# Attention with normalized Q and K on one core: a new plan for three engines, with 64-row QK matmuls, VectorE's QK placed first and one tile more for VectorE

## Chip, core and metric

The kernel runs on one core of a Trainium2 chip. The metric is the device time in microseconds (us). The kernel before takes 748.66 us (median of 3 runs, 748.62 to 749.63). All comparisons are made with runs of the kernel before on the same chip, in the same rounds; between chips and rounds its mean lies between 748.7 and 749.7 us in this study, so a ratio says more than a time.

## The reference

```python
B, H, S, Dh = 1, 32, 2048, 20
def reference(q, k, v, t):
    qn = q / (jnp.sqrt((q * q).sum(axis=-1, keepdims=True)) + 1e-6)
    kn = k / (jnp.sqrt((k * k).sum(axis=-1, keepdims=True)) + 1e-6)
    logits = jnp.einsum('bhqd,bhkd->bhqk', qn, kn) * t[None, :, None, None]
    attn = softmax(logits, axis=-1)
    return jnp.einsum('bhqk,bhkd->bhqd', attn, v)
```

Inputs and output are bfloat16. The logits are bounded, so no maximum is taken. There are 32 x 2048 x 2048 exponentials, and they are the bulk of the work.

## The kernel before

The program builds a list of tasks with durations and dependencies, runs a list scheduler over it at build time, and emits each engine's instructions in the order that came out. On the chip each engine then works strictly in that order. So the durations in the plan never appear in the program; they only decide the order.

```python
SEM_LAT = {"PE": 0.18, "ACT": 0.15, "DVE": 0.10, "POOL": 0.15, "SP": 0.0}
...
if e == "PE":     # prefer the kind of matmul that ran last: a change of kind costs time
    x = min(ready[e], key=lambda r: (r[0] + (0.0 if r[2].name[:2] == last_pe[0] else self.SWITCH), r[1]))
```

The work of a head is 16 row tiles of 128 keys, each with four units of 128x512 logits. Most tiles are ScalarE's: three units make a wave in three PSUM banks (psA, double buffered), and one exp instruction of 128x1536 turns it into bfloat16 probabilities in the ring p_ring. Some tiles are VectorE's: it reads the logits of one unit at a time from the single bank psD (L532, four times per tile) and makes the exponential in integer arithmetic, in four wide instructions per tile (L540 to L546).

```python
DVE_TILES = [4 if h % 3 == 1 else 3 for h in range(H)]      # 107 tiles for VectorE
...
def add_wave(w):          # QK of three units: a 64-row pair, and a single at 128 rows
    pair = ...            # two units whose operands lie in different halves of the array
    qks = [add("PE", ..., lambda e, tk, part=part:
               f_qk(e, part, 32 if plain else 64 if part is pair else 128), ...,
               deps, due_a(us[0]) - 100) for part in parts]
    act[w] = add("ACT", f"exp{w}", ..., 0.065 + n / 1200.0, qks + war, w)   # n = 1536
...
def add_dgroup(jg):       # VectorE's tile: QK into psD, then L532, four times
    for g in reversed(range(NG)):
        qk = add("PE", f"qkD{j}.{g}", ... qk_mm(e, h, r, g, psD[:, :], 128 if j else 32),
                 PE_MM, dep, due - 0.5)
        t1_prev[0] = add("DVE", f"t1.{j}.{g}", ...)          # L532
```

The operand of a 128-row QK is padded with zeros (qz), so 64 and 128 rows give the same result. PV of both kinds of tiles accumulates in the single bank psO, four matmuls of 32 columns at a time. At the end of a head VectorE transposes psO (L446), and the next head's PV waits for that.

Of the kernel before, what the change touches and what calls it, by code (L numbers as in the profile page):

```python
# [27 lines left out]

class Task:
    __slots__ = ("eng", "fn", "dur", "deps", "pri", "name", "lat", "dma", "n", "users",  # L30
                 "start", "end", "seq", "inc", "cnt")

    def __init__(self, eng, name, fn, dur, deps, pri, lat=0.0, dma=None):
        self.eng, self.name, self.fn, self.dur = eng, name, fn, dur
        self.deps = [d for d in deps if d is not None]
        self.pri, self.lat, self.dma = pri, lat, dma
        self.inc, self.cnt = False, 0


class Program:  # L40



    SEM_LAT = {"PE": 0.18, "ACT": 0.15, "DVE": 0.10, "POOL": 0.15, "SP": 0.0}

    SWITCH = 0.3

    def __init__(self):
        self.tasks = []
# [5 lines left out]
        return t  # L55

    def schedule(self):
        for t in self.tasks:
            t.users = []
        for i, t in enumerate(self.tasks):  # L60
            t.seq = i
            deps = []
            for d in t.deps:
                deps += d() if callable(d) else [d]
            t.deps = list(dict.fromkeys(deps))
            t.n = len(t.deps)
            for d in t.deps:
                d.users.append(t)
        free = {}
        ready = {}  # L70
        events = []
        rt = {}

        def arrive(t, when):
            heapq.heappush(events, (when, 0, t.seq, t))

        for t in self.tasks:
            free.setdefault(t.eng, 0.0)
            ready.setdefault(t.eng, [])
            rt[t.seq] = 0.0  # L80
            if t.n == 0:
                arrive(t, 0.0)
        order = {e: [] for e in free}
        done = 0
        last_pe = [""]
        while events:
            now = events[0][0]
            touched = set()
            while events and events[0][0] <= now:
                _, kind, _, t = heapq.heappop(events)  # L90
                touched.add(t.eng)
                if kind == 0:
                    heapq.heappush(ready[t.eng], (t.pri, t.seq, t))
            for e in touched:
                if free[e] > now + 1e-9 or not ready[e]:
                    continue
                if e == "PE":
                    x = min(ready[e], key=lambda r: (r[0] + (0.0 if r[2].name[:2] == last_pe[0] else self.SWITCH), r[1]))
                    ready[e].remove(x)
                    heapq.heapify(ready[e])  # L100
                    t = x[2]
                else:
                    _, _, t = heapq.heappop(ready[e])
                t.start = now
                t.end = now + t.dur
                if e == "PE":
                    kind = t.name[:2]
                    if kind != last_pe[0]:
                        t.end += 0.09
                        self.nsw += 1  # L110
                    last_pe[0] = kind
                free[e] = t.end
                order[e].append(t)
                done += 1
                heapq.heappush(events, (t.end, 1, t.seq, t))
                for u in t.users:
                    lat = t.lat if t.dma else (0.0 if u.eng == e and e != "DVE" else self.SEM_LAT[e])
                    rt[u.seq] = max(rt[u.seq], t.end + lat)
                    u.n -= 1
                    if u.n == 0:  # L120
                        arrive(u, rt[u.seq])
        assert done == len(self.tasks), "dependence cycle"
        self.order = order
        return order
# [57 lines left out]
def bass_standalone__qk_norm__prompt_kernel(  # L182
# [20 lines left out]
    GD = 1  # L203
    WPLAIN = 5
    EARLY = 3
    NSOLO = 4
    LEAD = 2.1
    PE_MM = 0.23
    DVE_TILES = [4 if h % 3 == 1 else 3 for h in range(H)]

    with ExitStack() as es:  # L211
        sbuf = lambda name, shape, dt: es.enter_context(nc.sbuf_tensor(name, shape, dt))
# [107 lines left out]
        def add_prep(hs):  # L320
            due = hs[0] - LEAD
            n = len(hs)
            w = 2 * R * n

            def dv(name, fn, dur, deps):
                return add("DVE", name + str(hs[0]), fn, dur, deps, due)
            sums = []
            for i, h in enumerate(hs):
                x = qk_sb[h % NB]
                s1 = dv("sq", lambda e, tk, x=x: e.tensor_tensor(sq[:, :, :], x[:, :, :], x[:, :, :], ALU.mult),  # L330
                        0.86, lds[h] + last_sum)
                sums.append(dv("sum", lambda e, tk, i=i: e.tensor_reduce(  # L332
                    rs["sum"][:, 2 * R * i:2 * R * (i + 1)], sq[:, :, :], AXIS_X, ALU.add), 0.86, [s1] + prep_last[0]))
                last_sum[:] = sums[-1:]
            c = dv("rs", lambda e, tk: e.tensor_scalar(  # L335
                rs["u"][:, 0:w].bitcast(I32), rs["sum"][:, 0:w].bitcast(I32), -0.5, 1597463007.0, ALU.mult, ALU.add),
                0.11 + 0.03 * n, sums)
            cur = rs["u"]
            for tgt in (rs["y"], rs["r"]):
                c = dv("rs", lambda e, tk, cur=cur: e.tensor_tensor(  # L340
                    rs["a"][:, 0:w], cur[:, 0:w], cur[:, 0:w], ALU.mult), 0.09 + 0.03 * n, [c])
                c = dv("rs", lambda e, tk: e.scalar_tensor_tensor(
                    rs["b"][:, 0:w], rs["a"][:, 0:w], -0.5, rs["sum"][:, 0:w], ALU.mult, ALU.mult), 0.09 + 0.03 * n, [c])
                c = dv("rs", lambda e, tk, cur=cur, tgt=tgt: e.scalar_tensor_tensor(
                    tgt[:, 0:w], rs["b"][:, 0:w], 1.5, cur[:, 0:w], ALU.add, ALU.mult), 0.09 + 0.03 * n, [c])
                cur = tgt
            rq = rs["r"][:, 0:w].rearrange("p (n x) -> p n x", n=n)[:, :, 0:R]
            tq = t_f32[:, hs[0]:hs[0] + n]
            tq = bass.AP(tq.tensor, tq.offset, [tq.ap[0], [1, n], [0, R]])
            c = dv("rs", lambda e, tk: e.tensor_tensor(rq, rq, tq, ALU.mult), 0.08 + 0.03 * n, [c, tcp])  # L350
            if hs[0] == 0:
                first_head(c)
                prep_last[0] = [norm[0]] + rot[0][-1].deps
# [1 line left out]
            for i, h in enumerate(hs):  # L355
                x, b = qk_sb[h % NB], h % NN
                war = [trn[h - NN]] if h >= NN else [z_qkn[b]]
                norm[h] = dv("norm", lambda e, tk, x=x, b=b, i=i: e.tensor_tensor(  # L358
                    qkn[b][:, :, 0:D], x[:, :, :], bc(rs["r"][:, 2 * R * i:2 * R * (i + 1)], 2 * R), ALU.mult),
                    0.86, [c] + war)  # L360
            prep_last[0] = [norm[h] for h in hs]
            for h in hs:
                add_trn(h)
# [17 lines left out]
        def first_head(rinv):  # L381
# [1 line left out]
            kv = kx[:, :].rearrange("p (e c g w) -> p e c g w", e=4, c=4, g=4)  # L383
            nk = add("DVE", "normk0", lambda e, tk: e.tensor_tensor(
                kx[:, 0:512].rearrange("p (r w) -> p r w", w=32)[:, :, 0:D],
                x[:, R:2 * R, :], bc(rs["r"][:, R:2 * R], R), ALU.mult), 0.45, [rinv, z_kx], -3)

            rq = rs["r"][:, 0:R]
            nq = add("DVE", "normq0", lambda e, tk: e.tensor_tensor(
                qkn[0][:, 0:R, :].rearrange("p (c g) w -> p c g w", g=4)[:, :, :, 0:D],  # L390
                x[:, 0:R, :].rearrange("p (g c) d -> p c g d", c=4),
                bass.AP(rq.tensor, rq.offset, [rq.ap[0], [1, 4], [4, 4], [0, D]]), ALU.mult),
                0.45, [rinv, z_qkn[0]], -2.9)
            cp = []
            for dl in range(1, 4):
                for (g0, s0, m) in ((0, dl, 4 - dl), (4 - dl, 0, dl)):
# [46 lines left out]
        def add_fin(h):  # L443
# [2 lines left out]
            trO[h] = add("DVE", f"tr{h}", lambda e, tk: e.transpose(  # L446
                oT[:, :, :].rearrange("p r d -> p (r d)"), psO[:, :]), 0.63,
                [lambda: pv_users[h]] + ([fin[h - 1]] if h else []), -10 + due)
            rc = add("DVE", f"rec{h}", lambda e, tk: e.reciprocal(rec[:, :], oT[:, :, D]), 0.17, [trO[h]], due)
            st = o_stage[b2][:, :].rearrange("p (r d) -> p r d", d=D)  # L450
            src, rb = oT[:, :, 0:D], bc(rec[:, :], R)
            if h == 0:
# [1 line left out]
                src = oT[:, :, 0:D].rearrange("p (c m) d -> p c m d", m=4)  # L454
                rb = bass.AP(rec, 0, [rec[:, :].ap[0], [4, 4], [1, 4], [0, D]])
            fin[h] = add("DVE", f"fin{h}", lambda e, tk: e.tensor_tensor(st, src, rb, ALU.mult),
                         0.45, [rc] + (sto[h - 2] if h >= 2 else []), due)
            if h == 0:
                sto[h] = [dma("SP", "st0", bass.AP(out.tensor, out[0, 0].offset + 4 * g * D,
                                                   [[16 * D, 32], [512 * D, 4], [1, 4 * D]]),  # L460
# [10 lines left out]
        def add_wave(w):  # L471
# [17 lines left out]
            for h in hs:  # L489
                moved = any(A_units[u][0] == h and (A_units[u][1] - A_units[u][2]) % 4 for u in us)  # L490
                deps += [trn[h]] + (rot[h] if h or moved else rot[h][:1]) + ([] if h or plain else qz0)
            qks = [add("PE", f"q{'2' if part is pair else 'k'}A{w}", lambda e, tk, part=part: f_qk(e, part, 32 if plain else 64 if part is pair else 128),
                       PE_MM * (1 if plain or part is pair else len(part)), deps, due_a(us[0]) - 100) for part in parts]
            for h in hs:
                qk_users[h] += qks
            p0 = us[0] % NP
# [1 line left out]
            war = [pv_of_group[(u - NP) // 4] for u in us if u >= NP]  # L498
            act[w] = add("ACT", f"exp{w}", lambda e, tk: e.activation(  # L499
                p_ring[:, p0 * 512:p0 * 512 + n], psA[:, slot * WAVE * 512:slot * WAVE * 512 + n], ACT.Exp),  # L500
                0.065 + n / 1200.0, qks + war, w)

        def add_group(i):
            us = list(range(4 * i, 4 * i + 4))
# [12 lines left out]
        def add_dgroup(jg):  # L517
# [5 lines left out]
            for i, j in enumerate(js):  # L523
                h, r = D_tiles[j]
                due = h + (j - d0[h] + 0.3) / DVE_TILES[h] - 0.25
                for g in reversed(range(NG)):
                    dep = [trn[h]] + rot[h] + (qz0 if h == 0 and j else []) + [t1_prev[0]]
                    qk = add("PE", f"qkD{j}.{g}", lambda e, tk, h=h, r=r, g=g, j=j: qk_mm(
                        e, h, r, g, psD[:, :], 128 if j else 32), PE_MM, dep, due - 0.5)
                    qk_users[h].append(qk)  # L530
                    o = 2048 * i + 512 * g
                    t1_prev[0] = add("DVE", f"t1.{j}.{g}", lambda e, tk, o=o: e.tensor_scalar(  # L532
# [3 lines left out]
            x = xt[sx][:, 0:w]  # L536

            def dv(name, fn, dur, deps):
                return add("DVE", f"{name}{js[0]}", fn, 0.075 + dur * len(js), deps, due)
            te = dv("e", lambda e, tk: e.tensor_scalar(  # L540
                ee[se][:, 0:w], x, 0x7C00, KE_BITS, ALU.bitwise_and, ALU.bitwise_or), 0.533, t1s + old("e", NE))
            t5 = dv("s", lambda e, tk: e.tensor_scalar(  # L542
# [93 lines left out]
```

## Time and profile before

| Reading | Value | Where |
|---|---|---|
| time, span of the profiled run | 748.66 us, 746.8 us | runs, page |
| exps of ScalarE | 540 | groups |
| first exp starts, last exp ends | 14.60 us, 742.72 us | trace |
| VectorE busy | 714.2 us | page |
| tiles of VectorE | 107 | kernel |

From the page: the span, the busy time of the engines (time, share, number of instructions), and the chain that ended last, by engine.

```profile
span 746.8 us, 12310 instructions
...
PE 672.8 (90%) x4862; PEld 191.9 (26%) x4952; DVE 714.2 (96%) x1201; ACT 727.8 (97%) x542; POOL 9.2 (1%) x24
...
ACT 93%; DVE 2%; DMA 2%; PE 1%; SPq 1%; issue 0%; ACTq 0%
```

Three engines look full, but the chain goes through ScalarE alone for 93% of the span. The costliest groups (line, engine, operation, tiles, number, then busy us, mean ns of one, idle time before them and what ended it). PE is TensorE, PEld its weight loads, DVE VectorE, ACT ScalarE; a line such as L499 is a line of the program:

```profile
L499 ACT ACTIVATE p_ring<-psA 128x1536 bf16<-128x1536 f32 x540 | 726.3, 1668 | 13.7 <-PE psA L425 13.7
L425 PE MATMUL psA<-qz,kR 64*128 64x512 bf16 (+1 forms) x1170 | 305.0, 388 | 26.2 <-ACT p_ring L499 18.9
L532 DVE TENSOR_SCALAR xt<-psD 128x512 int16<-128x512 f32 x428 | 293.0, 685 | 20.3 <-PE psD L425 13.9
```

540 exps of 1668 ns would be 901 us, but they cover 726 us. So the records of neighbouring exps overlap, by some 0.32 us, and a pause shorter than that does not show as idle time. The timeline of ScalarE, with unbroken runs of exps merged (start, length, number, idle time before):

```profile
14.60 2.79 ACT L499 ACTIVATE p_ring<-psA 128x1536 bf16<-128x1536 f32 x2 [11.91 <-PE psA L425]
17.63 4.35 ACT L499 ACTIVATE p_ring<-psA 128x1536 bf16<-128x1536 f32 x3 [0.23 <-PE psA L425]
22.68 1.45 ACT L499 ACTIVATE p_ring<-psA 128x1536 bf16<-128x1536 f32 x1 [0.70 <-PE psA L425]
24.73 52.50 ACT L499 ACTIVATE p_ring<-psA 128x1536 bf16<-128x1536 f32 x39 [0.60 <-PE psA L425]
77.45 665.28 ACT L499 ACTIVATE p_ring<-psA 128x1536 bf16<-128x1536 f32 x495 [0.21 <-PE psA L425]
```

The same stretch in the chain of waits, and the length of single exp records (minimum, median, maximum in ns) in the view of the tile p_ring:

```profile
77.45 663.93 ACT p_ring L499 x494
```

```profile
L499 ACT ACTIVATE p_ring<-psA x540: 1444/1676/1852, 14.6 to 741.0; 128x1536 bf16<-128x1536 f32 x180
```

TensorE's slots and modes can be read from the timeline of the kernel before, around 302 us:

```profile
302.07 0.39 PE L425 MATMUL psA<-qz,qkT 64*128 64x512 bf16 x2
...
302.39 0.39 PE L425 MATMUL psA<-qz,kR 128*128 128x512 bf16 x1
...
302.71 0.40 PE L434 MATMUL psO<-p_ring,vaug 128*32 128x512 bf16 x4
```

A pair of 64 rows, a single of 128 rows and a PV of four column groups follow each other at 0.32 us, where a matmul that keeps the mode follows at about 0.22 (two PVs in a row, for example: median 0.226 us over 213 pairs of this trace). Last, VectorE's longest wait (us in total, times, longest):

```profile
DVE xt L532 <- PE psD L425: 13.9, 29, 1.2
```

### The profile page before, as it was taken

The page shows a single profiled execution, that of the slowest core. Times are in us where ns is not written, and L with a number is a line of the kernel's source. Part 1 is how long each engine was busy: PE and PEld are TensorE (multiplying, and loading weights), DVE is VectorE, ACT ScalarE, POOL GpSimd, SP SyncE. Part 2 cuts the span into 40 slices and gives each one's busy share as a digit, 9 for nine tenths or more (in the row PEclk, how much of TensorE's full clock was granted, in tenths as well). Part 3 has the DMA queues.
Part 4 walks back from the last instruction along what each step waited for, and adds up shares of the span by engine and source line. Part 5 has one row for each costly group of instructions (what it writes and reads, how often), then busy time and mean ns, then how long its engine had stood idle before and what let it go on. Part 6 is the DMA issues. An engine that isn't in the chain of part 4 may idle for free.

```text
span 746.8 us, 12310 instructions
## 1 busy us (share of the span) xinstructions
PE 672.8 (90%) x4862; PEld 191.9 (26%) x4952; DVE 714.2 (96%) x1201; ACT 727.8 (97%) x542; POOL 9.2 (1%) x24
## 2 busy tenths in 40 slices
PE   1998999899999999998999999989999998999997
PEld 0222222222222222222222222222222222222221
DVE  7899999999999999999999999999999999999997
ACT  2999999999999999999999999999999999999997
POOL 4000000000000000000000000000000000000000
PEclk9999999999999999999999999999999999999999
DMA  5533241332403324241342404324132341413000
GB/s 74 82 44 57 35 74 18 81 41 61 56 5 80 42 64 53 36 77 14 75 43 51 69 7 91 27 65 56 34 69 25 69 48 35 77 15 89 7 5 5
DMA packets 197929, 36.49 MB, mean 49 GB/s; under 512 B 173680, under 2 KB 197872, under 8 KB 197872
## 3 DMA queue, kind: packets, MB, share of 16 engines
q1 hardware_dynamic: 197728, 35.62, 29.9%
q8 instruction: 39, 0.64, 0.4%
q14 instruction: 18, 0.15, 0.1%
q10 hardware_dynamic: 144, 0.08, 0.0%
HBM read 7.87 MB, written 2.62 MB: 14 GB/s over the span
## 4 chain that ended last, share of the span: by engine, by line
ACT 93%; DVE 2%; DMA 2%; PE 1%; SPq 1%; issue 0%; ACTq 0%
ACT p_ring L499 93%; SPq L244 1%; PE psA L425 1%; DMA kR<-kx 1%; DMA qk_sb<-in_q_dram 1%; DVE sq L330 0%; PE psD L425 0%; DVE xt L532 0%; PE psO L434 0%; DMA qkT<-qkn 0%; DMA qk_sb<-in_k_dram 0%; DVE rs_sum L332 0%; ACTq L211 0%; DVE tt L546 0%; DVE rs_u L335 0%
## 5 line engine op out<-in xcount | busy, mean ns | idle before, releaser
L499 ACT ACTIVATE p_ring<-psA 128x1536 bf16<-128x1536 f32 x540 | 726.3, 1668 | 13.7 <-PE psA L425 13.7
L425 PE MATMUL psA<-qz,kR 64*128 64x512 bf16 (+1 forms) x1170 | 305.0, 388 | 26.2 <-ACT p_ring L499 18.9
L532 DVE TENSOR_SCALAR xt<-psD 128x512 int16<-128x512 f32 x428 | 293.0, 685 | 20.3 <-PE psD L425 13.9
L434 PE MATMUL psO<-p_ring,vaug 128*32 128x512 bf16 x1620 | 151.8, 388 | 3.9 <-DVE oT L446 1.8
L425 PEld LDWEIGHTS psA<-qz,kR 64*128 64x128 bf16 (+1 forms) x1212 | 83.6, 94 | 228.6 <-ACT p_ring L499 118.8
L425 PE MATMUL psA<-qz,qkT 64*128 64x512 bf16 (+1 forms) x382 | 124.1, 387 | 6.8 <-ACT p_ring L499 4.4
L546 DVE TENSOR_TENSOR tt<-xt,mm 128x2048 f16<-128x2048 f16 x107 | 130.0, 1215 | 0.2
L425 PE MATMUL psD<-qz,kR 128*128 128x512 bf16 x292 | 112.4, 385 | 9.3 <-DVE xt L532 4.6
L540 DVE TENSOR_SCALAR ee<-xt 128x2048 int16<-128x2048 int16 x107 | 72.7, 680 | 0.7
L544 DVE TENSOR_SCALAR mm<-xt 128x2048 int16<-128x2048 int16 x107 | 73.2, 684 | 0.0
L542 DVE TENSOR_SCALAR ss<-xt 128x2048 int16<-128x2048 int16 x107 | 73.0, 683 | 0.0
L434 PEld LDWEIGHTS psO<-p_ring,vaug 128*32 128x32 bf16 x1620 | 39.2, 94 | 85.5 <-issue 71.1
L425 PEld LDWEIGHTS psA<-qz,qkT 64*128 64x128 bf16 (+1 forms) x393 | 31.3, 94 | 71.1 <-ACT p_ring L499 38.7
L425 PEld LDWEIGHTS psD<-qz,kR 128*128 128x128 bf16 x318 | 30.7, 97 | 55.4 <-DVE xt L532 34.5
L434 PE MATMUL psO<-tt,vaug 128*32 128x512 f16 x428 | 42.4, 387 | 2.5 <-DVE tt L546 1.9
L434 PE MATMUL psO<-ss,vaug 128*32 128x512 f16 x428 | 42.5, 388 | 1.4 <-DVE ss L542 0.5
L434 PE MATMUL psO<-ee,vaug 128*32 128x512 f16 x428 | 42.6, 388 | 1.1 <-DVE ee L540 0.8
L425 PE MATMUL psD<-qz,qkT 128*128 128x512 bf16 x95 | 36.6, 385 | 3.3 <-issue 1.1
L330 DVE TENSOR_TENSOR sq<-qk_sb 128x640 f32<-128x640 bf16 x32 | 27.4, 857 | 3.3 <-DMA qk_sb<-in_q_dram 3.3
L332 DVE TENSOR_REDUCE rs_sum<-sq 128x32 f32<-128x640 f32 x32 | 25.9, 808 | 0.1
L358 DVE TENSOR_TENSOR qkn<-qk_sb,rs_r 128x640 bf16<-128x640 bf16 x31 | 25.2, 817 | 0.1
L446 DVE STREAM_TRANSPOSE oT<-psO 128x512 f32<-128x512 f32 x32 | 22.7, 711 | 1.4 <-PE psO L434 1.2
(36 smaller groups left out, 119.4 us busy)
## 6 DMA issues: line engine op xcount, KB each, us to landing
kR<-qkT SPq DMA_DIRECT2D x62, 96.0 KB, 2.1
qz<-qkT SPq DMA_DIRECT2D x128, 32.0 KB, 1.9
kR<-qkT SPq DMA_DIRECT2D x62, 64.0 KB, 2.0
qk_sb<-in_k_dram SPq DMA_DIRECT2D x32, 80.0 KB, 2.1
vaug<-in_v_dram SPq DMA_DIRECT2D x32, 80.0 KB, 3.3
qk_sb<-in_q_dram SPq DMA_DIRECT2D x124, 20.0 KB, 2.5
out_dram<-o_stage SPq DMA_DIRECT2D x31, 80.0 KB, 1.6
kR<-qkT SPq DMA_DIRECT2D x62, 32.0 KB, 1.9
```

The source lines that it names most:

```text
L330: s1 = dv("sq", lambda e, tk, x=x: e.tensor_tensor(sq[:, :, :], x[:, :, :], x[:, :, :], ALU.mult), 0.86, lds[h] + last_sum)
L332: sums.append(dv("sum", lambda e, tk, i=i: e.tensor_reduce(rs["sum"][:, 2 * R * i:2 * R * (i + 1)], sq[:, :, :], AXIS_X, ALU.add), 0.86, [ ...
L358: norm[h] = dv("norm", lambda e, tk, x=x, b=b, i=i: e.tensor_tensor(qkn[b][:, :, 0:D], x[:, :, :], bc(rs["r"][:, 2 * R * i:2 * R * (i + 1) ...
L425: return eng.matmul(dst, lhsT, mov, tile_position=(p0, 0))
L434: last = eng.matmul(psO[32 * g:32 * g + 32, :], vaug[h % NV][:, r_of(g), :], rhs_of(g), start=start, stop=False, skip_group_check=True, ti ...
L446: trO[h] = add("DVE", f"tr{h}", lambda e, tk: e.transpose(oT[:, :, :].rearrange("p r d -> p (r d)"), psO[:, :]), 0.63, [lambda: pv_users[h ...
L499: act[w] = add("ACT", f"exp{w}", lambda e, tk: e.activation(p_ring[:, p0 * 512:p0 * 512 + n], psA[:, slot * WAVE * 512:slot * WAVE * 512 + ...
L532: t1_prev[0] = add("DVE", f"t1.{j}.{g}", lambda e, tk, o=o: e.tensor_scalar(xt[sx][:, o:o + 512], psD[:, :], X_MUL, X_ADD, ALU.mult, ALU.a ...
L540: te = dv("e", lambda e, tk: e.tensor_scalar(ee[se][:, 0:w], x, 0x7C00, KE_BITS, ALU.bitwise_and, ALU.bitwise_or), 0.533, t1s + old("e", NE))
L542: t5 = dv("s", lambda e, tk: e.tensor_scalar(ss[se][:, 0:w], x, float(SHIFT - 4096), None, ALU.add), 0.533, t1s + old("s", NE))
L544: tm = dv("m", lambda e, tk: e.tensor_scalar(mm[sm][:, 0:w], x, 0x3FF, 0x3800, ALU.bitwise_and, ALU.bitwise_or), 0.533, t1s + old("m", NM))
L546: tT = dv("T", lambda e, tk: e.tensor_tensor(tt[se][:, 0:w], x.bitcast(FP16), mm[sm][:, 0:w].bitcast(FP16), ALU.mult), 1.067, [tm] + old(" ...
```

## The change

The intent: give the scheduler durations that the trace shows; put VectorE's QK matmuls ahead of ScalarE's waves, so that VectorE waits less for psD; use 64 rows for the singles and for VectorE's QK too, so that TensorE changes mode less often; and return to 128 rows where a window of 3.41 us of the plan has little TensorE work, to keep the clock up. Heads are prepared singly, their small operations spread in time, matmuls in the first 25 us are planned at double length (PE_REST), and VectorE gets 108 tiles instead of 107. The diff, cut to its core:

```diff
-    SEM_LAT = {"PE": 0.18, "ACT": 0.15, "DVE": 0.10, "POOL": 0.15, "SP": 0.0}
+    SEM_LAT = {"PE": 0.20, "ACT": 0.17, "DVE": 0.14, "POOL": 0.15, "SP": 0.0}
+    LIGHT = 30.0
+    TICK = 3.41
+    LOAD = 3072.0
+    PASSES = 10
+    PE_REST = 25.0
 ...
     def schedule(self):
+        heavy = set()
+        choice = [t for t in self.tasks if t.rows == 0]
+        for _ in range(self.PASSES):
+            for t in choice:
+                t.rows = 128 if t in heavy else 64
+                t.name = ("qk" if t in heavy else "q2") + t.name[2:]
+            self.list_schedule()
+            pe = [t for t in self.order["PE"] if t.end > self.LIGHT]
+            more, i, load = set(), 0, 0.0
+            for j, t in enumerate(pe):
+                while pe[i].end < t.end - self.TICK:
+                    load -= pe[i].work or 4.0 * pe[i].rows
+                    i += 1
+                if load < self.LOAD and i:
+                    more.update(x for x in pe[i:j] if x.work == 0 and x.rows == 64)
+                load += t.work or 4.0 * t.rows
+            if not more:
+                break
+            heavy |= more
+        return self.order
 ...
-    NSOLO = 4
-    LEAD = 2.1
+    NSOLO = 32
+    LEAD = 2.7
+    SPREAD = 0.6
 ...
-    DVE_TILES = [4 if h % 3 == 1 else 3 for h in range(H)]
+    DVE_TILES = [4 if h % 8 in (1, 4, 6) else 3 for h in range(H)]
 ... (durations of VectorE's preparation: 0.86 to 0.735 and the like)
-            qks = [add("PE", ..., f_qk(e, part, 32 if plain else 64 if part is pair else 128), ...
+            qks = [add("PE", ..., f_qk(e, part, tk.rows), ...
+            for x, part in zip(qks, parts):
+                x.rows = 32 if plain else 64 if part is pair else 0 if len(part) == 1 else 128
 ...
-                0.065 + n / 1200.0, qks + war, w)
+                0.052 + n / 1200.0, qks + war, w)
 ...
-                        e, h, r, g, psD[:, :], 128 if j else 32), PE_MM, dep, due - 0.5)
+                        e, h, r, g, psD[:, :], tk.rows), PE_MM, dep, due - 100.05)
+                    qk.rows, qk.work = 0 if j else 32, 0
```

## The prediction

> **What bounds it now.** ScalarE: the chain of waits is 93% ACT L499 (exp of a 128x1536 wave) and nothing else from 77.45 us to the last exp. In the timeline the first exp starts at 14.60 us, the last ends at 742.72, and the span ends 4.1 us later. The page shows only 1.8 us of ScalarE idle after the first exp, too little: the records overlap. From their start times, the median interval between exps is 1.331 us, the mean 1.348. Over 539 intervals the excess is 9.3 us: 2.2 before 26 us, 0.8 between 50 and 80, about 6.3 in later stalls of 0.03 to 0.5 us. That is what a better order can win. VectorE is busy 714 us (96%), but its slots (starts, not overlapping records) add up to about 697 us: some 40 us of slack. TensorE looks 90% busy; in the timeline a QK pair of 64 rows takes a slot of 0.32 us, a 128-row single 0.32, a PV of four 0.32, against 0.22 for a matmul that follows its own mode: about 0.1 us per change of mode. The Trainium skill, "TensorEngine Tiling (Array Packing)", Key Properties, says that a change of mode drains TensorE; this trace agrees.
>
> **What the change does.**
> 1. VectorE gets 108 tiles, not 107: 1616 units for ScalarE, not 1620 (538 waves of three, one of two): -1.75 us, all on the critical path.
> 2. The tile costs VectorE 5.3 us (4x0.60 + 3x0.60 + 1.13); heads prepared singly instead of in pairs cost about 8 us in small operations. Slots rise to about 711 us, slack falls to 20 to 25: still behind ScalarE, barely.
> 3. 64-row singles and psD tiles remove a change of mode in most waves (roughly 50 us of TensorE in all), and halves can overlap, so waves are ready earlier.
> 4. VectorE's QK ahead of waves: fewer waits of DVE L532 for psD (13.9 us, 29 times in the waits), at up to 0.3 us before a wave.
> 5. 64-row matmuls lower TensorE's activity. The Trainium skill, "TensorE: Matmul & The Clock Gate", Part 1, says activity over windows of 3413 ns sets the clock. Here the granted clock is 1.00 from 24.9 us to 745, and the lightest 3.41 us I count has six full matmuls' work (3072 column passes), just the plan's limit for 128 rows. I expect no throttling; it is the main risk.
>
> **Sum.** 748.66 - 1.75 (units) - 4 (of the small stalls) - 0.5 (before 80 us) + 0.6 (new waits on a tighter VectorE and psD first) = 743.0 us. Without any stall it would be about 737.6, so over 2% faster (733.7) is next to impossible. Range 739.5 to 748.0. Faster by over 2%: 0.01; within 2%: 0.95; slower by over 2%: 0.04.
>
> **What would show it.** 1: 539 exps. 2: rs operations 32 each, VectorE busy 720 us or more. 3: psA singles and psD mostly 64-row; mean exp interval 1.335 to 1.342. 4: DVE L532 waiting for psD under 10 us. 5: clock 0.99 or more. First exp still at 14.6 us, tail still 4 us.
>
> **What would make it wrong.** The clock halving in light stretches, each costing ScalarE a few us; VectorE becoming the bound; psD first delaying waves; or small stalls that do not come from changes of mode, so that only 1.75 us are won.

## The result and the profile after

| | before | after |
|---|---|---|
| median | 748.64 us (747.92 to 749.63, 4 runs) | 747.44 us (747.06 to 747.93, 4 runs) |
| span of the profiled run | 746.8 us | 745.3 us |
| exps | 540 | 539 |
| VectorE busy | 714.2 us | 722.0 us |

The ratio is 0.9983, with a 95% interval of 0.9966 to 1.0001. A ratio is the record's: it compares the fast runs of both kernels in the same rounds, and is not quite the ratio of the medians quoted here. In a second comparison, with more runs (experiment e5), it is 0.9977 (0.9964 to 0.9989). So the change gains about 0.2%, not the 0.75% that was predicted. All runs shown in this table are fast.

The page after, in the same three views as before (lines L539, L462 and L573 are L499, L425 and L532 of the kernel before):

```profile
span 745.3 us, 12530 instructions
...
PE 644.9 (87%) x4960; PEld 163.4 (22%) x4960; DVE 722.0 (97%) x1321; ACT 725.7 (97%) x541; POOL 9.2 (1%) x24
...
ACT 96%; DVE 2%; PE 1%; DMA 0%; issue 0%; ACTq 0%; SPq 0%
```

```profile
L539 ACT ACTIVATE p_ring<-psA 128x1536 bf16<-128x1536 f32 x539 | 724.2, 1775 | 14.2 <-PE psA L462 14.2
L462 PE MATMUL psA<-qz,kR 64*128 64x512 bf16 (+1 forms) x1209 | 292.0, 385 | 49.4 <-ACT p_ring L539 41.2
L573 DVE TENSOR_SCALAR xt<-psD 128x512 int16<-128x512 f32 x432 | 295.0, 683 | 11.2 <-PE psD L462 8.5
```

```profile
14.61 2.79 ACT L539 ACTIVATE p_ring<-psA 128x1536 bf16<-128x1536 f32 x2 [11.92 <-PE psA L462]
17.64 1.45 ACT L539 ACTIVATE p_ring<-psA 128x1536 bf16<-128x1536 f32 x1 [0.24 <-PE psA L462]
19.80 2.79 ACT L539 ACTIVATE p_ring<-psA 128x1536 bf16<-128x1536 f32 x2 [0.71 <-PE psA L462]
23.52 2.79 ACT L539 ACTIVATE p_ring<-psA 128x1536 bf16<-128x1536 f32 x2 [0.93 <-PE psA L462]
26.74 714.39 ACT L539 ACTIVATE p_ring<-psA 128x1536 bf16<-128x1536 f32 x532 [0.43 <-PE psA L462]
```

```profile
L539 ACT ACTIVATE p_ring<-psA x539: 1261/1787/1989, 14.6 to 739.9; 128x1536 bf16<-128x1536 f32 x180
```

```profile
DVE xt L573 <- PE psD L462: 8.5, 14, 1.1
```

TensorE did become less busy (672.8 to 644.9 us), it is idle longer waiting for ScalarE (41.2 us ahead of the psA matmuls in the second line, 18.9 in the kernel before), and VectorE waits less for psD. Everything that was meant to happen on TensorE and VectorE happened. Yet the intervals between starts of exps have the same mean as before (1.348 us) and nearly the same sum of short "stalls" after 80 us, 6.0 us before and 6.5 after (counted over each kernel's own median interval, 1.331 and 1.330 us).

**What the ends say.** Where an exp starts late, look at the end of the record too. These are neighbouring exps around one such "stall" in each kernel, taken from the start and length of the records in the trace (us):

```
kernel   start     length   end       start to start   end to end
before   160.563   1.743    162.306   1.331            1.344
before   161.894   1.755    163.649   1.331            1.343
before   163.393   1.599    164.992   1.499            1.343
before   164.740   1.595    166.335   1.347            1.343
after    158.021   1.877    159.898   1.330            1.344
after    159.575   1.667    161.242   1.554            1.344
after    160.921   1.663    162.584   1.346            1.342
```

The late start is matched by a shorter record, and the end comes as regularly as ever. The end of a record is a real event: ScalarE's semaphore rises 0.008 to 0.010 us after it, in every exp of both traces. In the stretch from 80 to 735 us the intervals between ends have the median 1.343 us, and in the trace of after all of them lie between 1.342 and 1.345. Starts follow at 1.331 us and so run ahead of the ends by 12 to 13 ns per exp (the record gets longer by that much each time), until the data of an exp come after that early point; then the start falls back and the lead begins anew. **The rate of ScalarE here is one exp per 1.343 us, and the sum of "late starts" is the sum of 12 ns leads given back. It is not lost time.** This is theory 1; the experiments below test it. The rival, theory 2, is the prediction's reading: a start every 1.331 us is possible, and late QK matmuls take it away (in the new kernel perhaps for a new reason, such as VectorE's QK standing in front).

With true gaps defined by the ends (the excess of an interval over 1.343 us), the whole difference of the two profiled runs adds up:

| Part | before | after | difference |
|---|---|---|---|
| exp work: one wave of three less, one wave of two (0.917) for one of three | 540 waves | 539 waves | -1.77 us |
| true gaps before 30 us | 2.08 | 2.74 | +0.66 |
| 30 to 80 us | 0.33 | 0.07 | -0.26 |
| 80 to 735 us | 0.38 | 0.16 | -0.22 |
| after the last exp | 4.12 | 4.13 | +0.01 |
| span | 746.84 | 745.26 | -1.58 |

The 0.16 us of after is what is left when 488 intervals of 1.3433 us are counted over a rounded 1.343, so it is no gap at all.

The +0.66 us sits where the clock is still half: the trace grants the full clock at 24.9 us before and at 28.1 us after. But it is not the later grant that makes it: after, e3, e5, e7 and e14, whose start is planned nearly alike, all have 2.73 to 2.75 us there, with the full clock at 28.0 to 31.3 us. What does go with the grant in these five is the part from 30 to 80 us: 0.01 us in e7 (28.0), 0.94 in e5 (30.7), 1.16 in e14 (31.3). So the table is the ledger of one pair of runs. In e5, a second profile of the kernel after, the two parts before 80 us are +1.28 us over before and a drop of the clock costs 0.96 us later; its span is 747.08 us, 0.24 us over the profiled run of before. The exp work is the part that stays.

### The profile page after: what moved, and what is told of

It reads as the page before. It is cut to its first block, busy times and chain, and to the rows that moved or that the text cites. A ratio compares the mean times of both kernels' runs of the same rounds, so it can differ in the third digit from the quotient of the medians.

```text
span 745.3 us, 12530 instructions
## 1 busy us (share of the span) xinstructions
PE 644.9 (87%) x4960; PEld 163.4 (22%) x4960; DVE 722.0 (97%) x1321; ACT 725.7 (97%) x541; POOL 9.2 (1%) x24
## 4 chain that ended last, share of the span: by engine, by line
ACT 96%; DVE 2%; PE 1%; DMA 0%; issue 0%; ACTq 0%; SPq 0%
ACT p_ring L539 96%; PE psA L462 1%; DVE sq L367 0%; DMA qk_sb<-in_k_dram 0%; DVE rs_sum L369 0%; PE psD L462 0%; PE psO L471 0%; DVE rs_u L372 0%; DVE rs_a L377 0%; ACTq L245 0%; DVE rs_b L379 0%; DVE kx L434 0%; DVE qkn L395 0%; DVE oT L483 0%; DVE xt L573 0%
## 5 line engine op out<-in xcount | busy, mean ns | idle before, releaser
L462 PE MATMUL psA<-qz,kR 64*128 64x512 bf16 (+1 forms) x1209 | 292.0, 385 | 49.4 <-ACT p_ring L539 41.2
L471 PE MATMUL psO<-p_ring,vaug 128*32 128x512 bf16 x1616 | 156.6, 388 | 2.4 <-ACT p_ring L539 1.3
L462 PE MATMUL psA<-qz,qkT 64*128 64x512 bf16 (+1 forms) x392 | 126.9, 383 | 15.4 <-ACT p_ring L539 12.7
L462 PE MATMUL psD<-qz,kR 64*128 64x512 bf16 (+1 forms) x321 | 123.2, 384 | 4.1 <-DVE xt L573 3.1
L462 PEld LDWEIGHTS psA<-qz,kR 64*128 64x128 bf16 (+1 forms) x1209 | 63.0, 93 | 180.1 <-ACT p_ring L539 163.3
L462 PEld LDWEIGHTS psD<-qz,kR 64*128 64x128 bf16 (+1 forms) x321 | 29.9, 93 | 73.9 <-DVE xt L573 45.4
L462 PE MATMUL psD<-qz,qkT 64*128 64x512 bf16 (+1 forms) x107 | 41.3, 386 | 2.3 <-DVE xt L573 1.9
```

What stands on the lines that cost most here:

```text
L462: return eng.matmul(dst, lhsT, mov, tile_position=(p0, 0))
L471: last = eng.matmul(psO[32 * g:32 * g + 32, :], vaug[h % NV][:, r_of(g), :], rhs_of(g), start=start, stop=False, skip_group_check=True, ti ...
```

## Experiments

Unless said otherwise a result is correct. All ratios are to the kernel before, in the same rounds.

| | Kernel | median us | before, median | ratio (95%) |
|---|---|---|---|---|
| e1 | before, no VectorE tiles (wrong) | 749.47 (one run 1674.86) | 749.73 | 0.9989 (0.9976 to 1.0003) |
| e2 | before, 108 tiles | 758.08 | 749.73 | 1.0115 (1.0100 to 1.0130) |
| e3 | after, 107 tiles | 749.91 | 749.73 | 0.9998 (0.9986 to 1.0011) |
| e4 | after, 128 rows in the start | 747.39 | 749.73 | 0.9966 (0.9952 to 0.9979) |
| e5 | after again | 748.16 | 749.73 | 0.9977 (0.9964 to 0.9989) |
| e6 | after, QK doubled in every second wave | 748.56 | 749.73 | 0.9986 (0.9972 to 1.0000) |
| e7 | after, 109 tiles, exp of 1.343 us in the plan | 746.36 | 749.73 | 0.9952 (0.9938 to 0.9965) |
| e8 | after, VectorE's QK last again | 769.40 | 749.73 | 1.0262 (1.0248 to 1.0276) |
| e9 | e7 and e4 | 746.69 | 749.38 | 0.9964 (0.9951 to 0.9976) |
| e10 | e1 again, for its profile | 749.58 | 749.38 | 1.0003 (0.9985 to 1.0022) |
| e11 | before, 108 tiles, new durations | 788.13 | 749.38 | 1.0523 (1.0496 to 1.0550) |
| e12 | after, 128 rows | 771.43 | 749.38 | 1.0298 (1.0282 to 1.0314) |
| e13 | after, 64 rows everywhere | 751.24 (747.91 to 760.18, all six runs) | 748.90 | 1.0014 (0.9999 to 1.0029) |
| e14 | after, exp of 1.343 us in the plan | 747.90 | 748.90 | 0.9981 (0.9969 to 0.9993) |
| e15 | after, 109 tiles | 746.42 | 748.90 | 0.9968 (0.9955 to 0.9981) |
| e16 | e7 with 110 tiles | 745.87 | 748.90 | 0.9957 (0.9946 to 0.9969) |

### Is the late start lost time? (e1, e10, e6)

**e1 and e10: take the load from TensorE and VectorE.** The kernel before, with VectorE's tiles left out and all other QKs at 128 rows. ScalarE has the same 540 waves. The result is wrong.

```diff
-            pair = [] if plain else next(
+            pair = [] if True else next(
...
-            while nj < len(D_groups) and D_groups[nj][0] < d0[h + 1]:
+            while False and nj < len(D_groups) and D_groups[nj][0] < d0[h + 1]:
```

Expected, e1:

> The kernel before without VectorE's tiles (their QK, exp arithmetic and PV left out: a wrong result on purpose), all QK at 128 rows; ScalarE still has the same 540 waves. TensorE and VectorE then have little to do, so no QK should be late. Theory 1 (ScalarE is full: its exps end every 1.343 us whatever TensorE does, and the start times run ahead of the ends): the spacing of ends stays at 1.343 us, only the true gaps before 80 us (2.4 us) can go, so 746 to 748.5 us against 748.6. Theory 2 (the prediction's: starts could come every 1.331 us and the 6 us of later excess is time lost to late QK): the spacing of exps falls to 1.331 us and the time to 742 us or less.

The profiled run of e1 was a slow one of its own kind: 1674.86 us. Its trace has matmuls of 512 columns 0.84 us apart where 0.21 is usual, throughout; TensorE stayed at a quarter of its speed and never left it. That run says nothing about the question. The other four took 748.38 to 749.61 us, up to 1.1 us over what theory 1 said, and far from the 742 of theory 2. e10 ran the same kernel for a profile at full clock.

> The kernel before without VectorE's tiles again, for a profile at full clock (the profiled run of the first time never left the slow clock and took 1674.86 us, the other four took 748.4 to 749.6). At full clock theory 1 expects ends 1.343 us apart with VectorE and TensorE nearly idle, starts 1.33 or 1.343 us apart, and about 748.5 us; theory 2 expects 1.331 us between ends and 742 us. The times of the first run already speak for theory 1.

Measured: 749.58 us. The page of e10 (busy), its long stretch on the timeline, and the lengths of exp records:

```profile
PE 567.8 (76%) x3178; PEld 155.7 (21%) x3240; DVE 156.0 (21%) x345; ACT 727.5 (97%) x542; POOL 9.2 (1%) x24
```

```profile
69.33 674.46 ACT L499 ACTIVATE p_ring<-psA 128x1536 bf16<-128x1536 f32 x502 [0.49 <-PE psA L425]
```

```profile
L499 ACT ACTIVATE p_ring<-psA x540: 1446/1770/1771, 14.1 to 742.0; 128x1536 bf16<-128x1536 f32 x180
```

With VectorE busy 21% of the time, ScalarE does 502 exps in 674.46 us. The first record of the stretch is about 1.45 us long, so the ends are (674.46 - 1.45) / 501 = 1.343 us apart, exactly as in the loaded kernels. The starts are 1.343 us apart here too, the records nearly all 1.77 us long. That is not because every wave is ready early. 471 of the 487 starts between 80 and 735 us come 20 to 30 ns after a semaphore of TensorE. The exp that ends at 301.827 us frees its half of psA, the three QKs of the wave that goes there begin at once, their semaphore rises at 302.718, and the exp of that wave starts at 302.743. The QKs:

```profile
301.88 0.82 PE L425 MATMUL psA<-qz,kR 128*128 128x512 bf16 x3 [0.19 <-ACT p_ring L499]
```

So the start is nearly always 0.916 us behind the end of the exp before the last, and the record fills the rest. This speaks against theory 2, for little is left on TensorE and VectorE and the rate stays, but it does not settle the matter alone: the loop through the double-buffered psA could itself set the rate, since (1.770 + 0.916) / 2 is 1.343 us. Two things speak against that loop. In the other kernels the same distance has other medians, 1.003 us in before and 0.887 in after, and the ends are 1.343 us apart all the same. And e6 lengthens it. (True gaps in this run: 4.2 us before 80 us, where the clock also dropped once, from 66.4 to 69.8 us, and 0.16 us from 80 to 735 us.)

**e6: make waves later.** If late starts cost time, more lateness must cost more.

```diff
                     last = qk_mm(eng, h, r, g, psA[...], rows)
+                if w % 2 == 0 and part is parts[-1] and w >= 30:
+                    last = qk_mm(eng, h, r, g, psA[...], rows)     # the same matmul once more
                 return last
```

> The kernel after, in which the single QK of every second wave from wave 30 on is issued twice (the same result written twice), so each of these waves is ready about 0.21 us later. From the trace of after: if every start later than 1.331 us behind the one before is lost time (theory 2), the loss after 80 us grows from 5.5 to about 26 us, so about 768 us. If only a wave that comes after the previous exp has ended is lost (theory 1), it stays at 0, the records of exps only get shorter, the ends stay 1.343 us apart and the time stays within 1.5 us of after.

Measured: 748.56 us, 0.4 us over e5 in the same rounds (0.9986 against 0.9977, the intervals overlap), where theory 2 said 20 us more. The view of p_ring and the long stretch of e6:

```profile
L541 ACT ACTIVATE p_ring<-psA x539: 1104/1557/1777, 14.6 to 740.7; 128x1536 bf16<-128x1536 f32 x180
```

```profile
26.73 715.08 ACT L541 ACTIVATE p_ring<-psA 128x1536 bf16<-128x1536 f32 x532 [0.43 <-PE psA L462]
```

The median record is 1.557 us instead of 1.787, and the median distance from an end to the start of the next exp but one is 1.126 us instead of 0.887: the waves do come later and the starts lose their lead, but the stretch of 532 exps is only 0.7 us longer than in after (714.39), and the ends are still 1.343 us apart in the median. Theory 2 falls here, and the loop through psA with it. So waves could come 0.2 us later, at least every second one, at next to no cost to ScalarE, which is why taking changes of mode off TensorE could not speed up the exps.

### What is the rest of the change worth? (e5, e3, e2, e11, e8, e12)

**e5: the kernel after, again.**

> The kernel after, unchanged, to narrow its interval and to be timed beside the next three. The ledger by ends (units -1.77, start +0.66, 30 to 80 us -0.26, later -0.22) says 1.2 to 1.8 us under before, ratio 0.998. The prediction's 743.0 would be a ratio of 0.9925.

Measured: 748.16 against 749.73 us, ratio 0.9977. In its profiled run the clock was half from 566.6 to 570.0 us, which cost 0.96 us of true gaps there.

**e3: the kernel after with the old 107 tiles** (`DVE_TILES = [4 if h % 3 == 1 else 3 ...]`).

> The kernel after with the old 107 tiles (heads 1, 4, 7, ... have four). Theory 1: all the rest of the change is worth nothing or less (+0.66 us in the cold start, -0.5 us later), so 748.5 to 749.2 us, equal to before. Theory 2 in its later form (64-row QK and new order did remove lost time, something else gave it back): the same time could hold, but then the spacing of ends would differ between the kernels; theory 1 says 1.343 us in both.

Measured: ratio 0.9998. Without the 108th tile, the whole change shows no gain, and ends are 1.343 us apart in this run as well, with 0.16 us of true gaps from 80 to 735 us.

**e2: the kernel before with only the 108 tiles** (`DVE_TILES = [4 if h % 8 in (1, 4, 6) else 3 ...]`).

> The kernel before with 108 VectorE tiles instead of 107 and nothing else. Theory 1: the four units less are the whole gain of the change, so about -1.8 us (746.9), if the old plan, which thinks VectorE slower than it is, still orders it well; its own plan has VectorE ending last, so up to +3 us is possible and would say that the new durations are needed for the 108th tile. Theory 2: the same -1.8 us, no more.

Measured: 758.08 us, 8.4 us over before. This was a miss beyond the 3 us allowed. The trace shows true gaps of 8.2 us from 80 to 735 us, and 9.1 us after the last exp instead of 4.1: VectorE ends last.

**e11: the kernel before with 108 tiles and the new durations**, with the old priorities, rows and paired preparation.

```diff
-    DVE_TILES = [4 if h % 3 == 1 else 3 for h in range(H)]
+    DVE_TILES = [4 if h % 8 in (1, 4, 6) else 3 for h in range(H)]
     (and all durations and latencies of the change; nothing else of it)
```

> The kernel before with 108 tiles and the new durations in the plan, but with the old order of VectorE's QK, 128-row singles, paired preparation. If the new durations alone made the 108th tile bearable, the time is 746.9 to 748 us. If VectorE's QK first and the 64 rows are needed, VectorE ends last and the time is 755 us or more (758.1 with the old durations; the plan itself now sees its delays and puts ScalarE's last exp late).

Measured: 788.13 us. The new durations alone make it worse than the old ones did.

**e8: VectorE's QK behind the waves again**, in the kernel after.

```diff
-                        e, h, r, g, psD[:, :], tk.rows), PE_MM, dep, due - 100.05)
+                        e, h, r, g, psD[:, :], tk.rows), PE_MM, dep, due - 0.5)
```

> The kernel after with VectorE's QK back behind the waves (due - 0.5 instead of due - 100.05), still 108 tiles. If putting them first is what lets VectorE carry the 108th tile (fewer waits for psD), its waits for psD rise well above 8.5 us, VectorE ends last, and the time goes 5 us or more over before. If the order of these QKs is worth nothing, the time stays at that of after.

Measured: 769.40 us. Its waits of VectorE for psD and of ScalarE (us in total, times, longest):

```profile
DVE xt L573 <- PE psD L462: 18.1, 26, 1.4
```

```profile
ACT p_ring L539 <- PE psA L462: 14.7, 6, 11.9
ACT p_ring L539 <- PE psO L471: 12.1, 7, 2.9
```

The waits for psD are more than twice those of after, and ScalarE has a wait that after does not have: 12.1 us for PV into psO. That is VectorE being late: psO is not handed over to the next head before VectorE's last tile and transpose, so PV stops, p_ring fills and the exps stop. The trace bears it out: six of the seven gaps over 0.3 us after 30 us end 0.5 to 0.7 us after such a transpose (ScalarE pauses from 376.4 to 379.28 us, for example, and the transpose runs from 378.06 to 378.77). After the last exp it takes 12.9 us instead of 4.1.

**e12: no 64-row singles and no 64-row QK for VectorE**, in the kernel after.

```diff
-                t.rows = 128 if t in heavy else 64
-                t.name = ("qk" if t in heavy else "q2") + t.name[2:]
+                t.rows = 128
+                t.name = "qk" + t.name[2:]
```

> The kernel after with all single QKs and all QKs of VectorE at 128 rows (only the 64-row pairs stay), still 108 tiles and VectorE first. If the 64 rows are worth nothing, 747.4 to 748.2 us as after. If the tiles' QK can only be had in time without changes of mode, VectorE falls behind as its plan says and the time is 5 us or more over before. The clock should be 1.0 throughout, in every run, since no stretch is light.

Measured: 771.43 us, with the same new wait and VectorE's waits for psD at 15.1 us; 14.4 us after the last exp.

```profile
ACT p_ring L539 <- PE psA L462: 13.6, 6, 11.5
ACT p_ring L539 <- PE psO L471: 12.1, 5, 3.0
```

Together: at 108 tiles, each of the two parts is needed, and undoing either costs over 20 us; at 107 tiles they show no gain (e3). They do not make ScalarE faster. They let VectorE carry one tile more, and that is worth 1.77 us. (Undoing a part also changes the plan's whole order and the choice of rows, so the 20 us is what the part is worth within this scheduler, not a cost of its own.)

### The clock (e13, e4, e9)

**e13: no return to 128 rows in light stretches** (`LOAD = 0.0`).

> The kernel after with 64 rows in all single QKs and all of VectorE's QKs, no return to 128 rows in light stretches. If the return guards the clock, the clock drops to half in several stretches (lightest window under 2560 passes), the granted clock is lower than after's 0.996 to 0.999 and the time rises 1 us or more over after's 748.2. If it guards nothing, 747.5 to 748.5 us and the same clock.

Measured: six runs from 747.91 to 760.18 us, with a mean granted clock of 0.974 to 0.994 (the two of 0.974, at 760.18 and 759.41 us, count as slow, since they are over 1.5% above the fastest, and are left out of the ratio; the four fast ones lie between 747.91 and 751.57). Windows of its profile: length, busy us of PE, PEld, DVE, ACT and POOL, the granted clock, the DMA share and GB/s.

```profile
222.00:226.00 4.00, 2.52 (x20) 0.62 (x16) 4.00 (x8) 4.00 (x5) 0.00 (x0) 1.00 0.45 49
226.00:230.00 4.00, 3.99 (x24) 0.82 (x27) 2.89 (x9) 3.06 (x4) 0.00 (x0) 0.57 0.35 21
540.00:550.00 10.00, 8.86 (x47) 1.53 (x43) 8.04 (x16) 8.71 (x7) 0.00 (x0) 0.68 0.00 0
```

A light stretch of TensorE (2.52 us of 4) is followed by one at half clock, and ScalarE has 1.05 us of true gaps there; the trace has three such drops, of 3.4, 3.4 and 10.2 us, between 80 and 735 us, and 5.2 us of true gaps. So the return to 128 rows earns its place: it gives no time, but without it even the four fast runs have a ratio of 1.0014 against e5's 0.9977, and the intervals do not meet. (The two slow runs have the lowest clock, but no trace of them was kept, so what they lost is not shown to be the same thing.) The guard is not complete: in e5's profile the clock still dropped once.

**e4: 128 rows for the singles of the first 30 us**, in the kernel after.

```diff
             self.list_schedule()
+            if not heavy:
+                first = {t for t in choice if t.end <= self.LIGHT}
+                if first:
+                    heavy |= first
+                    continue
```

> The kernel after, with the single QKs of the first 30 us at 128 rows as in the kernel before, so that TensorE has as much work there. If the 64-row QKs put off the moment at which the clock is granted in full (28.1 us after, 24.9 us before), the clock is full again at about 25 us, ScalarE's gaps before 30 us fall from 2.7 to about 2.1 us and the time by about 0.6 us to 746.8. If the later full clock has to do with the order alone, the clock comes at 28 us again and the time stays at 747.4.

Measured: the true gaps before 30 us fell to 2.15 us as expected, but the full clock came at 27.6 us, not 25 (in e12, at 128 rows too, it came at 28.0), and in the profiled run (750.07 us) it was half again from 44.6 to 51.5 us, and the true gaps from 30 to 80 us were 3.9 us. The other four runs took 746.85 to 747.64 us. The ratio, 0.9966, and that of e5, 0.9977, have overlapping intervals.

**e9: the same together with e7.**

> The 109-tile kernel planned with 1.343 us per exp, and the single QKs of the first 30 us at 128 rows. Theory 1: ScalarE's units and its true gaps are all that counts. Gaps before 30 us fall from 2.7 to about 2.1 us as in the warm-start run, so about 0.6 us under the 109-tile kernel (746.2): 745.6, ratio to before 0.994 to 0.995. If the clock drops in the light stretch near 40 us, as it did in the profiled warm-start run, up to 4 us of that run are lost.

Measured: 746.69 us, ratio 0.9964; e7 alone has 0.9952. The full clock came at 25.2 us and the gaps before 30 us fell to 2.03 us, but the clock dropped from 42.2 to 45.6 us and the gaps from 30 to 80 us rose to 2.9 us. What the start gained was given back 20 us later, so this part is not settled and is not recommended.

### Where to go from here (e14, e15, e7, e16)

The change plans an exp with 0.052 us plus 1536 / 1200 us, 1.332 us: the spacing of starts. With the spacing of ends, 1.343, the plan stays beside the real ScalarE for the whole run instead of being 6 us ahead at its end (11 ns x 539).

```diff
-                0.052 + n / 1200.0, qks + war, w)
+                0.063 + n / 1200.0, qks + war, w)                         # e14, e7, e16
...
-    DVE_TILES = [4 if h % 8 in (1, 4, 6) else 3 for h in range(H)]
+    DVE_TILES = [4 if h % 8 in (1, 4, 6) or h == 18 else 3 for h in range(H)]        # e15, e7
+    DVE_TILES = [4 if h % 8 in (1, 4, 6) or h in (10, 18) else 3 for h in range(H)]  # e16
```

e14, the duration alone:

> The kernel after with 1.343 us per exp in the plan and nothing else (108 tiles). Theory 1: ScalarE's ends after 80 us have almost no true gaps in after (0.2 to 1.1 us), so there is 0 to 1 us to win: 747.2 to 748.2.

Measured: 747.90 us, ratio 0.9981, that of after. No effect of its own is shown.

e15, the 109th tile alone:

> The kernel after with the 109th tile and the old exp duration of 1.332 us. Theory 1: four units less are -1.79 us if VectorE keeps up: 746.4. Its plan thinks ScalarE faster than it is, so VectorE looks tighter than it is and some of it may be lost: 746.4 to 748.

Measured: 746.42 us, ratio 0.9968, 1.5 us under e14 of the same rounds; 5.1 us after the last exp instead of 4.1.

e7, both:

> The kernel after, planned with 1.343 us for an exp of 1536 columns (the spacing of ends) instead of 1.332, and with a 109th VectorE tile (head 18). Theory 1: the plan no longer runs ahead of ScalarE by 11 ns per wave, 6 us at the end, and four units less give -1.8 us as long as VectorE keeps up: 745 to 746.5 us, 1 to 2 us under after. Theory 2: nothing is known to be gained from a slower duration; -1.8 us at most. If VectorE is now at its limit, a longer tail and no gain.

Measured: 746.36 us, ratio 0.9952, 1.8 us under e5 of the same rounds. The line of its long stretch:

```profile
26.73 712.70 ACT L539 ACTIVATE p_ring<-psA 128x1536 bf16<-128x1536 f32 x531 [0.43 <-PE psA L462]
```

The first record is about 1.45 us and the last wave, a single unit, ends 0.49 us after the one before; with these, 529 intervals take (712.70 - 1.45 - 0.49) / 529 = 1.344 us, and the tail is 4.1 us. This kernel is faster than both kernels: all its runs (745.35 to 746.67 us) lie under all of e5's (747.04 to 748.97), though the intervals of the two ratios just touch (0.9965 and 0.9964). Against e15, the 109th tile with the old duration, it shows no gain: 746.36 and 746.42 us.

e16, a 110th tile:

> The 109-tile kernel with a 110th tile (head 10), 1.343 us per exp in the plan. If ScalarE still bounds, another -1.8 us: 744.4. If VectorE is at its limit (its plan has 4.7 us of gaps on ScalarE against 2.1 with 109), no gain: 746 to 748, with true gaps between the ends after 80 us.

Measured: 745.87 us, ratio 0.9957. The expected 744.4 did not come: in the profiled run there are 1.7 us of true gaps from 80 to 735 us, the longest for psO, that is for VectorE. Within the intervals it equals e7. VectorE is now busy 727.9 us, 98% of the span, so the way of moving units to it ends here.

## Why the prediction was wrong

1. **The bound was named rightly, its rate was not.** "From their start times, the median interval between exps is 1.331 us, the mean 1.348. Over 539 intervals the excess is 9.3 us ... That is what a better order can win" is the step that failed, and with it the term "- 4 (of the small stalls)". Measured by ends, the kernel before has 2.8 us of true gaps in all (2.08 before 30 us, 0.33 and 0.38 later); after 80 us the change won 0.22 us where 4 were expected. e6 shows that waves 0.2 us later cost next to nothing where 20 us were at stake, and e10 has the same 1.343 us between ends with VectorE's tiles gone. The prediction's own list of what would make it wrong came near: "small stalls that do not come from changes of mode, so that only 1.75 us are won". But these stalls were no lost time at all. The trace offered the check: the chain's own stretch of 494 exps in 663.93 us gives 1.344 us each, and the mean over a long unbroken stretch is the rate.
2. **"Without any stall it would be about 737.6"** follows from the same error. With true gaps it is 748.64 - 1.77 - 2.8 = 744.1 us.
3. **Units, -1.75 us: right**, -1.77 measured in the ledger, and e3 (0.9998 without the tile, with an interval of 0.0013 to either side) shows no gain from the rest of the change.
4. **"- 0.5 (before 80 us)" had the wrong sign**: +0.40 in the profiled runs (+0.66 - 0.26). The plan has all choices before 30 us at 64 rows, and ScalarE's gaps there grew by 0.66 us; with 128 rows in the start they were 2.15 us (e4) and 2.03 us (e9), one profile each. The prediction did not look at the start for this. It is not shown that the rows also put off the full clock (28.1 us instead of 24.9): e4 had 27.6 and e12 28.0 with 128 rows, e9 25.2.
5. **"+ 0.6 (new waits on a tighter VectorE and psD first)" did not come**: no interval of after between 80 and 735 us is over 1.345 us, and VectorE's waits for psD fell from 13.9 to 8.5 us, as step 4 of the prediction said (under 10).
6. **Step 3's mechanism was right, its place was not.** TensorE was relieved (28 us less busy; e12, back at 128 rows, has 673.2 us again), but the path from there to ScalarE had slack already. What the relief bought was VectorE's capacity (e8, e12), which is used only through the number of tiles.
7. **The clock, as predicted**: 1.0 in the profiled run, 0.996 to 1.0 over all ten runs of after (four here, six in e5). The named risk is real (e13), and the guard answers most of it (one drop in e5). The prediction's figure of 3072 passes for the lightest window came from a trace in which some matmul records of psA and psD were missing (53 of 1620 for psA), so it was too low. The trace of after, complete for psA and psD, has a window of 2560 at 562.2 us without a drop; in e5, the same kernel, the window at 563.0 us counts 2560 too (21 QK records of that trace are missing) and the clock dropped at 566.6 us. No sharp limit is shown by these runs.

The sum of the four terms as measured: -1.77 (units) + 0.40 (before 80 us) - 0.22 (later) + 0.01 (tail) = -1.58 us of span; between the medians of the first runs it is -1.2 us, in e5 -1.6 us. That the terms outside the units nearly cancel is partly luck: in the profiled run of e5 they do not (above).

What stays open: what sets the 1.343 us inside ScalarE, and why record starts run ahead of the ends by 12 ns per exp; where exactly the clock's limit lies; and whether a start with more TensorE work can be had without the drop near 45 us.

## What to carry to other kernels

Before a better order is credited with time on a saturated engine, measure that engine's rate over a long unbroken stretch (length over count), or between the ends of its records: here the intervals between starts were shorter than the engine could sustain, and what they gave back later looked like stalls. To settle such a doubt, delay the supposed culprit on purpose, as e6 does. When an engine is full and has few true gaps (2.8 us here), little is left to gain but fewer instructions or less work on it; relief elsewhere counts only as capacity to take work from it, so test it together with moving that work, and once without. In e13 a lighter TensorE also met a dropping clock, so count its work per window when matmuls are made smaller.

## What the Trainium skill lacked or had wrong

- "Perfetto Trace Analysis", "Optimizing Scalar/DVE Operations", gives about 51 ns of overhead per ScalarE operation on PSUM. With 0.833 ns per element ("ScalarE: Activation LUTs", where it is stated for all functions) 1536 elements would take an estimated 1280 + 51 = 1331 ns. That is the spacing of starts here (1.331 us), but the sustained rate is 1.343 us, 63 ns over 1280, in every trace but the one of e1 at a quarter clock.
- "Perfetto Trace Analysis", the summary of the profiler's window per engine, says that a ScalarE record runs from the start in the ALUs to the acknowledged write. It does not say that the record of one and the same instruction varies: here from 1.44 to 1.85 us before and up to 1.99 us after, with ends evenly spaced. Only the ends could be used as a clock of the engine.
- "TensorE: Matmul & The Clock Gate", Part 1, explains the clock by activity in windows of 3413 ns, but beyond how busy TensorE has been it does not say what counts as activity. Here drops lasted 3.4 us or a multiple of it (3.4, 6.8, 10.2), as the page's window would have it. In e13, with half-height matmuls, there were three although TensorE was "busy" 85% of the time, where the kernel after, with 128 rows in light stretches, stayed at 0.996 to 1.0. Half height is not the only way: e2 and e11, with the old rows, dropped after stretches in which TensorE was busy 1.81 us of 3.4 and 1.38 of 4.
- The same page mentions a clock stuck at a quarter for 50 us and more. Here one run of e1 seems to have stayed at a quarter for all of its 1673 us (matmuls 0.84 us apart instead of 0.21), and the profile's mean clock says 1.000 for it, since the trace holds no record of the clock at all.
- "TensorEngine Tiling (Array Packing)", Key Properties, says that a change of tiling mode drains TensorE, without a figure. Here it costs about 0.1 us (slots of 0.32 against 0.22 us).
